# Infini-attention plus ReGLU on one core: one pool of PSUM banks, the token gate on VectorE, the memory in column tiles, and a plan with rings, queue and load times

## The chip, the core and the metric

The kernel runs on one core of one Trainium2 chip. The metric is the device time of one execution, in microseconds (us). Each time below is the median of four executions (of seven for the kernel before in the experiments), with the range in brackets. The profile is of one execution, and its "span" runs from the first to the last recorded instruction, which is about 2 us shorter than the device time. Engine names are those of the profile: PE is the matrix engine (TensorE), PEld its weight loads, DVE is VectorE, ACT is ScalarE, POOL is GpSimd, and SP is the engine whose queue issues most DMA transfers.

A run is called slow when it is over 1.5% above the fastest of the same kernel. The medians and ranges are of all runs; the three fast runs of the changed kernel have a median of 291.39 us.

## The reference

There are 2048 tokens of 512 features. An attention with a compressive memory (32 heads of 16, four segments of 512 tokens) and a gated ReLU feed-forward (1792 wide) are computed on the same input, and a scalar gate for each token mixes them:

```python
g = sigmoid((x * gate_w).sum(-1, keepdims=True))       # token gate: one number per token
a = infini_attention(x, wq, wk, wv, wo, beta)
b = (relu(x @ W_gate) * (x @ W_up)) @ W_down
return g * a + (1 - g) * b

# infini_attention, for each segment s of 512 tokens and each head
p   = softmax(qs @ ks.T * scale + causal_mask)
o   = sigmoid(beta) * (phi(qs) @ M) / (phi(qs) @ z + 1e-6) + (1 - sigmoid(beta)) * (p @ vs)
M, z = M + phi(ks).T @ vs,  z + phi(ks).sum()          # the memory, used by the next segment
```

## The kernel before

The kernel does not leave the order of instructions to a compiler. It makes a list of tasks, each with an engine, an estimated duration in ns, a priority and what it needs. It then simulates the engines and emits each task when the simulation starts it. **The order on every engine is fixed by this plan.** On the chip each engine executes its own list strictly in that order, and semaphores hold an instruction until its inputs are there. If a duration in the plan is wrong, the order stays, and the engines wait.

```python
class Plan:
    def run(self):
        ...                                            # cut: count what each task waits for
        for t in sorted((t for t in ready if t.avail <= now), key=rank):
            if busy.get(t.eng, 0.0) > now:
                continue
            ...                                        # cut: find a free PSUM bank
            if mode.get(t.eng) != t.mode:              # PE changes its tiling: a drain
                t.dur += SWITCH + (126 if t.mode and mode.get(t.eng) else 0)
            t.start = now
            busy[t.eng] = now + t.dur
            t.done = now + t.dur + t.lat
            order.append(t)
```

The kernel uses eight banks of PSUM. Four of them, `sp`, only ever hold scores, 32-row tiles that fill all four at once. One exponential of 128x2048 empties them ("fill" below means one such block of score matmuls; there are 80). Four single banks, `wb`, take all else. "Row tiles" are four matmuls that run side by side, each on 32 rows of PE's array; "column tiles" are the same on 32 columns each. An "eviction" is the instruction, mostly on VectorE, that copies a finished bank to SBUF and so lets PE use the bank again.

```python
sp = psum.tile([P, 4, L], F32, name="sp")
wb = [psum.tile([P, L], F32, name=f"wb{b}") for b in range(4)]
```

The token gate is computed by PE. 16 one-column matmuls give the sums of a segment, and a small fp32 matmul with a 0/1 matrix moves the gate values from "token on partition" to "four blocks of 32":

```python
def gate_tasks(seg):
    def pe():
        for t in range(4):
            for ci in range(NC):
                nc.tensor.matmul(bank(sl)[:, t:t + 1],
                                 lhsT=xT[seg % 3][:, ci, t * P:(t + 1) * P],
                                 rhs=gw[:, ci:ci + 1], ...)
    a = plan.add("PE", 420, key, pe, ...)
    ...                                                # cut: clamp, exponential, 1/(1+r), block mask
    d = plan.add("PE", 300, key, lambda: nc.tensor.matmul(
        bank(rsl)[:, 0:16], lhsT=fold[:]..., rhs=rblk[:]..., start=True, stop=True), ...)
```

The memory update is 16 full-array matmuls of 136 columns at the end of each of the first three segments:

```python
def memory(seg):
    for g in range(NC):
        for t in range(4):
            lo = (g % 2) * 136
            nc.tensor.matmul(wb[sl.banks[g // 2]][:, lo:lo + 136],
                             lhsT=pK[i][:, t, g * P:(g + 1) * P],
                             rhs=Vp[i][:, t, 8 * g:8 * g + 8, 0:HW], ...)
```

The softmax here doesn't subtract the row's maximum and nothing guards it: scores larger than these inputs give would overflow.

Of the kernel before, what the change touches and what calls it, by code (L numbers as in the profile page):

```python
# [12 lines left out]
P = 128  # L13
# [12 lines left out]
SWITCH = 100.0  # L26
RQ = 5
RE = 8
RH = 16


class Task:




    def __init__(self, eng, dur, key, emit, deps=(), lat=100, need=None, frees=(), after=None,
                 mode=None):
        self.eng, self.dur, self.key, self.emit, self.mode = eng, dur, key, emit, mode
        self.deps = [d for d in deps if d is not None]  # L40
        self.lat, self.need, self.frees, self.after = lat, need, tuple(frees), after
        self.avail = 0.0


class Slot:
    def __init__(self, kind):
        self.kind, self.banks, self.left = kind, (), 0


class Plan:  # L50



    def __init__(self, nbanks):
        self.tasks = []
        self.free = {i: 0.0 for i in range(nbanks)}

    def add(self, *a, **k):
        t = Task(*a, **k)
        self.tasks.append(t)  # L60
        return t

    def pick(self, slot, now):
        ok = [b for b in sorted(self.free) if self.free[b] is not None and self.free[b] <= now]
        if slot.kind == 2:
            for b in ok:
                if b % 2 == 0 and b + 1 in ok:
                    return (b, b + 1)
            return None
        for b in ok:  # L70
            if b ^ 1 not in ok:
                return (b,)
        return (ok[-1],) if ok else None

    def run(self):
        users = {}
        for t in self.tasks:
            t.wait = len(t.deps) + (t.after is not None)
            for d in t.deps:
                users.setdefault(id(d), []).append(t)  # L80
            if t.after is not None:
                users.setdefault(id(t.after), []).append(t)
            for s in t.frees:
                s.left += 1
        ready = [t for t in self.tasks if t.wait == 0]
        busy, mode = {}, {}
        now, order = 0.0, []
        left = len(self.tasks)
        while left:
            progressed = True  # L90
            while progressed:
                progressed = False
                def rank(t):
                    turn = t.mode and mode.get(t.eng) and t.mode != mode[t.eng]
                    return (bool(turn), t.key)
                for t in sorted((t for t in ready if t.avail <= now), key=rank):
                    if busy.get(t.eng, 0.0) > now:
                        continue
                    if t.need is not None and not t.need.banks:
                        got = self.pick(t.need, now)  # L100
                        if got is None:
                            continue
                        t.need.banks = got
                        for b in got:
                            self.free[b] = None
                    if mode.get(t.eng) != t.mode:
                        t.dur += SWITCH + (126 if t.mode and mode.get(t.eng) else 0)
                        mode[t.eng] = t.mode
                    t.start = now
                    busy[t.eng] = now + t.dur  # L110
                    t.done = now + t.dur + t.lat
                    order.append(t)
                    ready.remove(t)
                    left -= 1
                    for s in t.frees:
                        s.left -= 1
                        if s.left == 0:
                            for b in s.banks:
                                self.free[b] = t.done
                    for u in users.get(id(t), ()):  # L120
                        u.wait -= 1
                        u.avail = max(u.avail, t.start + t.dur if u.after is t else t.done)
                        if u.wait == 0:
                            ready.append(u)
                    progressed = True
            if not left:
                break
            times = [t.avail for t in ready if t.avail > now]
            times += [b for b in busy.values() if b > now]
            times += [f for f in self.free.values() if f is not None and f > now]  # L130
            assert times, "the plan is stuck"
            now = min(times)
        self.end = max(t.done for t in order)
        return order
# [3 lines left out]
def kernel(  # L138
# [21 lines left out]
    rpool = ctx.enter_context(tc.tile_pool(name="rpool", bufs=3))  # L160
    psum = ctx.enter_context(tc.tile_pool(name="psum", bufs=1, space=bass.MemoryType.PSUM))

    def sb(shape, dtype, name):
        return wpool.tile(shape, dtype, name=name)


    xT = [sb([P, NC, L], BF16, f"xT{i}") for i in range(3)]
    wq_sb = sb([P, NC, D], BF16, "wq_sb")
# [6 lines left out]
    gw = sb([P, NC], BF16, "gw")  # L175
    betab = sb([P, H], BF16, "betab")

    E = [sb([P, 4, L], BF16, f"E{i}") for i in range(RE)]
    x0 = E[RE - 1]
    clock = [3300.0]  # L180
    plan = Plan(4)

    def arrival(nbytes):
        clock[0] += nbytes / 340.0
        return plan.add("in%d" % len(plan.tasks), 0.0, 0.0, None, lat=clock[0])

    def load(eng, dst, src, nbytes):
        eng.dma_start(out=dst, in_=src)
        return arrival(nbytes)

    def load_cols(eng, t, ap, c0, c1):
        k = ap.shape[0] // P
        return load(eng, t[:, :, c0:c1], ap.rearrange("(c p) n -> p c n", p=P)[:, :, c0:c1],
                    k * P * (c1 - c0) * 2)

    def load_xT(seg):
        nc.sync.dma_start_transpose(out=xT[seg % 3][:], in_=x[seg * L:(seg + 1) * L, :])
        return arrival(L * D * 2 * 1.3)

    FP = [(0, 512), (512, 1024), (1024, 1408), (1408, F)]  # L200
    got_x, got_g, got_u = {}, {}, {}
    def load_halves(dst, src, k, nbytes):
        src = src.rearrange("(c p) n -> p c n", p=P)
        nc.sync.dma_start(out=dst[:, 0:k // 2], in_=src[:, 0:k // 2])  # L204
        nc.scalar.dma_start(out=dst[:, k // 2:k], in_=src[:, k // 2:k])
        return arrival(nbytes)

    got_x0 = load_halves(x0, x[0:L, :], 4, L * D * 2)
    got_q = [load_halves(wq_sb, A_wq, NC, D * D * 2)] * 2
    got_k = [load_cols(nc.sync, wk_sb, A_wk, 0, D)] * 2  # L210
    got_v = load_cols(nc.scalar, wv_sb, A_wv, 0, D)
    nc.scalar.dma_start(out=betab[:], in_=A_beta.partition_broadcast(P))
    with nc.allow_non_contiguous_dma(reason="1 KB"):
        nc.scalar.dma_start(out=gw[:], in_=gate_w.rearrange("(c p) -> p c", p=P))
    got_gw = arrival(0)

    def load_gu(i):
        got_g[i] = load_cols(nc.sync, wg_sb, B_W_gate, *FP[i])
        got_u[i] = load_cols(nc.sync, wu_sb, B_W_up, *FP[i])

    def load_wd(a, b):
        return load(nc.sync, wd_sb[:, a:b, :],
                    B_W_down.rearrange("(c p) n -> p c n", p=P)[:, a:b, :], (b - a) * P * D * 2)

    load_gu(0)
    load_gu(1)
    got_x[1] = [load_xT(1)]
    load_gu(2)
    load_gu(3)
    got_d = [load_wd(0, 7), load_wd(7, NF)]  # L230
    got_o = load_cols(nc.sync, wo_sb, A_wo, 0, D)
    got_x[2] = [load_xT(2)]


    junk = sb([P, L], BF16, "junk")
    nc.vector.memset(junk[:], 0.0)
# [16 lines left out]

    fold = sb([P, 4, 32], F32, "fold")
    nc.gpsimd.memset(fold[:], 0.0)
    pbm = sb([P, 4], F32, "pbm")
    nc.vector.memset(pbm[:], 0.0)
    for b in range(4):
        nc.gpsimd.affine_select(out=fold[:], in_=fold[:], compare_op=ALU.not_equal, fill=1.0,
                                base=-32 * b, pattern=[[0, 4], [-1, 32]], channel_multiplier=1)  # L260
        nc.vector.memset(pbm[32 * b:32 * b + 32, b:b + 1], 1.0)
    rblk = sb([P, 4, 4], F32, "rblk")
# [5 lines left out]
    grc = [sb([P, NC, 2, 2, 16], F32, f"grc{i}") for i in range(2)]  # L268

# [13 lines left out]

    sp = psum.tile([P, 4, L], F32, name="sp")
    wb = [psum.tile([P, L], F32, name=f"wb{b}") for b in range(4)]
    QT = [sb([P, L], BF16, f"QT{i}") for i in range(RQ)]
    KTe = [sb([P, L], BF16, f"KTe{i}") for i in range(RQ)]
    KTo = [sb([P, L], BF16, f"KTo{i}") for i in range(RQ)]
    pqT = [sb([P, L], BF16, f"pqT{i}") for i in range(RQ)]
    pK = [sb([P, 4, D], BF16, f"pK{i}") for i in range(2)]  # L290
    Vp = [sb([P, 4, H, 18], BF16, f"Vp{i}") for i in range(2)]
    oT = [sb([P, NC, L], BF16, f"oT{i}") for i in range(2)]
    hT = [sb([P, L], BF16, f"hT{i}") for i in range(RH)]
    T = [sb([P, 2, L], F32, f"T{i}") for i in range(2)]
    mbd = [sb([P, NC, 2, 4, 32], BF16, f"mbd{i}") for i in range(2)]
# [424 lines left out]
```

## Time and profile before

| | before |
|---|---|
| device time, us | 282.57 (282.07 to 282.74) |
| span of the profiled run, us | 280.8 |
| PE, DVE, ACT busy, us | 272.8, 205.7, 196.6 |
| idle of PE between its blocks, us | 4.2 |
| tiling changes of PE | 193, each a drain of 0.09 to 0.11 us |

The idle of PE and the drains are read from start-to-start times of the matmuls in the trace: a matmul of 512 columns is followed by the next after 216 ns when nothing is in the way. Idle counts each excess over 0.03 us beyond streaming and the usual drain; the 5.0 us of the prediction below counts the smaller ones too.

The first fence is the page of the kernel before: its span, the busy table, then two rows of busy tenths over 40 equal slices (9 is 90% or more), the granted clock of PE in tenths, and the shares of the chain of waits that ended last.

```profile
span 280.8 us, 5327 instructions
...
PE 272.8 (97%) x2122; PEld 113.4 (40%) x2122; DVE 205.7 (73%) x427; ACT 196.6 (70%) x176; POOL 87.6 (31%) x144
...
PE   8899999999989999999999999999999999999994
...
DVE  3588797798994768968997599957898966374221
...
PEclk9999999999999999999999999999999999999999
...
PE 92%; ACT 3%; DMA 3%; DVE 1%; issue 0%; SPq 0%; ACTq 0%
```

PE is full in every slice but the first two, one near 80 us and the last, and the chain of waits is PE for 92%. So time comes off this kernel only by taking work, drains or idle time from PE.

By start-to-start times a run of 16 one-column matmuls of the token gate takes 0.46 us, most often with a drain at its end. With the fold, the token gate costs PE 2.4 us in all. The three memory blocks cost 3.1 us. The last line is of the head gate, and will matter below: a small copy on 32 partitions, much like the 64 that the change adds, took 161 ns on VectorE.

The largest stall is early. In the timeline (start, duration, engine, line, operation; in brackets the idle time before it and what ended it) PE waits for `wk`, although two of its q projections, whose weights are there, are still to do:

```profile
9.55 1.25 PE L327 MATMUL wb<-xT,wk_sb 128*128 128x512 bf16 x5 [1.01 <-DMA wk_sb<-in_A_wk_dram]
```

The busy time of the engines in two stretches (stretch, its length, then busy us and number of instructions of PE, PEld, DVE, ACT and POOL, then the clock, the DMA share and GB/s):

```profile
0.00:115.00 115.00, 111.30 (x876) 46.26 (x877) 89.38 (x200) 87.69 (x82) 39.26 (x70) 1.00 0.38 101
115.00:275.00 160.00, 159.66 (x1240) 66.50 (x1239) 115.57 (x228) 108.88 (x95) 48.33 (x74) 1.00 0.04 12
```

### The profile page before, as it was taken

The numbers are of one execution on the slowest core, as the hardware profiler recorded it, in microseconds if no ns is written. First come the engines' busy times: TensorE is split into PE (matmuls) and PEld (weight loads), VectorE is DVE, ScalarE is ACT, GpSimd is POOL, SyncE is SP. The second block draws the span as 40 slices with busy tenths as digits, with TensorE's granted clock in tenths as the row PEclk, the third lists the DMA queues.
The fourth block names the chain that finished last, engine by engine and source line by source line (L and its number), as shares of the span: only waits on it lengthen the run. The fifth ranks groups of instructions, "written<-read, shape, count | busy, mean of one in ns | idle before, by whom it ended". The sixth has DMA issues, their size and how long they took to land.

```text
span 280.8 us, 5327 instructions
## 1 busy us (share of the span) xinstructions
PE 272.8 (97%) x2122; PEld 113.4 (40%) x2122; DVE 205.7 (73%) x427; ACT 196.6 (70%) x176; POOL 87.6 (31%) x144
## 2 busy tenths in 40 slices
PE   8899999999989999999999999999999999999994
PEld 3343444433434343343443344344434343444441
DVE  3588797798994768968997599957898966374221
ACT  3299797988886659888876779898897677723000
POOL 7014233334242332433343424443334243300000
PEclk9999999999999999999999999999999999999999
DMA  7999930013001010000001000000000010000011
GB/s 230 316 255 349 208 49 19 4 22 75 19 2 39 21 37 2 19 2 19 0 11 47 21 21 2 0 2 0 2 0 2 19 39 21 0 2 0 0 37 39
DMA packets 24488, 13.71 MB, mean 49 GB/s; under 512 B 13968, under 2 KB 24464, under 8 KB 24464
## 3 DMA queue, kind: packets, MB, share of 16 engines
q1 hardware_dynamic: 22720, 12.32, 16.5%
q10 hardware_dynamic: 1744, 1.06, 1.3%
q8 instruction: 16, 0.26, 0.4%
q14 instruction: 8, 0.07, 0.1%
HBM read 8.14 MB, written 2.10 MB: 36 GB/s over the span
## 4 chain that ended last, share of the span: by engine, by line
PE 92%; ACT 3%; DMA 3%; DVE 1%; issue 0%; SPq 0%; ACTq 0%
PE wb L327 73%; PE sp L478 9%; PE wb L518 7%; DMA wk_sb<-in_A_wk_dram 3%; ACT E L499 2%; PE wb L574 2%; PE wb L592 1%; ACT rg L628 1%; PE wb L360 1%; SPq L204 0%; DVE osb L658 0%; DVE T L547 0%; PE wb L380 0%; ACT e L416 0%; ACTq L628 0%
## 5 line engine op out<-in xcount | busy, mean ns | idle before, releaser
L499 ACT ACTIVATE E<-sp 128x2048 bf16<-128x2048 f32 x80 | 150.4, 1880 | 37.0 <-PE sp L478 33.0
L505 POOL TENSOR_SCALAR_AFFINE_SELECT E<-E 128x512 bf16<-128x512 bf16 x128 | 82.5, 660 | 156.0 <-ACT E L499 156.0
L327 PE MATMUL wb<-xT,wg_sb 128*128 128x512 bf16 x224 | 59.7, 380 | 0.0
L327 PE MATMUL wb<-xT,wu_sb 128*128 128x512 bf16 x224 | 59.3, 380 | 0.4 <-ACT rg L628 0.4
L327 PE MATMUL wb<-wd_sb,hT 128*128 128x512 bf16 x224 | 54.1, 380 | 0.0
L635 DVE TENSOR_TENSOR hT<-wb,rg 128x512 bf16<-128x512 f32 x56 | 38.1, 682 | 17.7 <-PE wb L327 9.7
L547 DVE STREAM_TRANSPOSE T<-wb 128x512 f32<-128x512 f32 x56 | 36.7, 693 | 14.9 <-PE wb L518 9.0
L628 ACT ACTIVATE rg<-wb 128x512 bf16<-128x512 f32 x56 | 33.0, 602 | 13.8 <-PE wb L327 13.8
L327 PEld LDWEIGHTS <-hT 128*128 128x128 bf16 x224 | 20.4, 98 | 26.1 <-issue 4.2
L327 PEld LDWEIGHTS <-wu_sb 128*128 128x128 bf16 x224 | 20.3, 98 | 26.2 <-issue 5.0
L327 PEld LDWEIGHTS <-wg_sb 128*128 128x128 bf16 x224 | 19.8, 98 | 25.3 <-issue 5.5
L658 DVE TENSOR_SCALAR osb<-wb,ngcol 128x512 bf16<-128x512 f32 x16 | 11.9, 741 | 17.7 <-PE wb L327 17.6
L558 DVE TENSOR_TENSOR o<-T,cf 128x512 bf16<-128x512 f32 x28 | 20.1, 718 | 1.0
L518 PE MATMUL wb<-E,Vp 128*17 128x256 bf16 (+3 forms) x512 | 20.4, 300 | 0.0
L478 PE MATMUL sp<-QT,KTo 32*128 32x512 bf16 (+3 forms) x256 | 17.1, 299 | 0.8 <-ACT E L499 0.8
L478 PE MATMUL sp<-QT,KTe 32*128 32x512 bf16 (+3 forms) x256 | 17.3, 302 | 0.3 <-ACT E L499 0.3
L327 PE MATMUL wb<-xT,wk_sb 128*128 128x512 bf16 x64 | 16.5, 380 | 1.0 <-DMA wk_sb<-in_A_wk_dram 1.0
L327 PE MATMUL wb<-wo_sb,oT 128*128 128x512 bf16 x64 | 17.1, 380 | 0.0
L327 PE MATMUL wb<-wv_sb,xT 128*128 128x512 bf16 x64 | 16.8, 380 | 0.2 <-DVE T L547 0.2
L327 PE MATMUL wb<-xT,wq_sb 128*128 128x512 bf16 x64 | 16.7, 380 | 0.1
L408 DVE CAST QT<-wb 128x512 bf16<-128x512 f32 x16 | 11.0, 688 | 6.8 <-PE wb L327 4.4
L518 PEld LDWEIGHTS <-Vp 128*17 128x17 bf16 x512 | 10.7, 91 | 13.0 <-issue 4.2
(70 smaller groups left out, 192.9 us busy)
## 6 DMA issues: line engine op xcount, KB each, us to landing
out_dram<-osb SPq DMA_DIRECT2D x16, 128.0 KB, 1.7
wd_sb<-in_B_W_down_dram SPq DMA_DIRECT2D x2, 896.0 KB, 8.4
wg_sb<-in_B_W_gate_dram SPq DMA_DIRECT2D x2, 512.0 KB, 9.6
wu_sb<-in_B_W_up_dram SPq DMA_DIRECT2D x2, 512.0 KB, 10.0
wg_sb<-in_B_W_gate_dram SPq DMA_DIRECT2D x2, 384.0 KB, 5.2
wu_sb<-in_B_W_up_dram SPq DMA_DIRECT2D x2, 384.0 KB, 5.2
wk_sb<-in_A_wk_dram SPq DMA_DIRECT2D x1, 512.0 KB, 7.7
wv_sb<-in_A_wv_dram ACTq DMA_DIRECT2D x1, 512.0 KB, 9.1
```

The source lines that it names most:

```text
L327: nc.tensor.matmul(bank(sl), lhsT=lhsT, rhs=rhs, start=(start and q == 0), stop=(stop and q == n - 1))
L408: prj["q", seg, c] = plan.add("DVE", 690, key - RQK, lambda: nc.vector.tensor_copy(QT[i][:], bank(sl)), [a], DVL, frees=[sl])
L478: nc.tensor.matmul(sp[:, j, off:off + n], lhsT=kt[32 * j:32 * j + 32, kb * P:(kb + 1) * P], rhs=QT[i][32 * j:32 * j + 32, kb * P:kb * P + ...
L499: b = plan.add("ACT", 1880, key, lambda Ef=Ef: nc.scalar.activation(Ef[:], sp[:], ACT.Exp, scale=SCALE), [a] + eread.get(n - RE, []), ACL)
L505: nc.gpsimd.affine_select(out=m, in_=m, compare_op=ALU.is_ge, fill=0.0, base=0, pattern=[[0, 4], [1, P]], channel_multiplier=-1)
L518: nc.tensor.matmul(wb[sl.banks[0]][32 * j:32 * j + HW, kb * P:kb * P + w], lhsT=Vp[i][:, kb, 8 * c + 2 * j + r, 0:HW], rhs=E[(5 * u + f) % ...
L547: done.append(plan.add("DVE", 700, key - RL, lambda r=r, sl=sl: nc.vector.transpose(T[m][:, r], bank(sl)), [a, att.get(("part", m, u - 1)) ...
L558: nc.vector.tensor_tensor(dst[0].rearrange("p (q r e) -> p r q e", r=2, e=DH), t[:, :, :, 0:DH], cf[:, :, :, None].to_broadcast([P, 2, 16, ...
L574: a = plan.add("PE", 216, key + r, lambda r=r, sl=sl: nc.tensor.matmul(bank(sl), lhsT=mbd[i][:, c, r].rearrange("p j e -> p (j e)"), rhs=p ...
L628: nc.scalar.activation(rg[0][:], bank(sl), ACT.Relu)
L635: nc.vector.tensor_tensor(hT[(NF * seg + fv) % RH][:], bank(sl), rg[0][:], ALU.mult)),
L658: nc.vector.tensor_scalar(osb[0][:], bank(sl), ngcol[:, tt:tt + 1], None, ALU.mult)
```

## The change

The intent was to take the small work off PE and to have a better plan. The diff is long; its core, with cuts marked, follows.

1. The token gate moves to VectorE: a multiply-and-sum pass over the rows of x, which are loaded a second time, and 16 small copies per segment in place of the fold matmul.
2. The memory becomes 64 column-tile matmuls of 34 columns, tied to a block of the probability-times-value product (PV), which uses column tiles too.
3. PSUM becomes one pool of eight banks. The four score banks may be lent to other work between fills.
4. The plan knows buffer rings, the sync queue and a table of measured load times. Many task durations are reduced. A block of column tiles is ranked later while PE is in row tiles, and a score fill may follow a PV block directly.
5. A table of 132 shifts, found by a search against the plan, changes the priority of single tasks.
6. The last output tile is computed in two halves.

```diff
+SHIFT = {
+    29: 30000, 32: 310000, 48: 80000, ...            # cut: 132 entries in all
+}
...
-    sp = psum.tile([P, 4, L], F32, name="sp")
-    wb = [psum.tile([P, L], F32, name=f"wb{b}") for b in range(4)]
+    plan.pool("ps", 8)
+    ps = psum.tile([P, 8 * L], F32, name="ps")
...
+    LANDS = dict(n0=4500, q=5950, k=9300, v=9750, g0=11800, u0=13300, gw=13700, g1=15200, u1=16700,
+                 x1=18400, g2=20400, u2=21600, g3=22800, u3=24000, d0=27700, d1=30400, o=31800)
...
+    plan.add("SP", 23300, -1e9, None)                # the sync queue is busy with loads until here
...
 def gate_tasks(seg):
-        a = plan.add("PE", 420, key, pe, got_x[seg] + [got_gw], PEL, need=sl)
+        for t in range(4):
+            zs.append(plan.add("DVE", 640, key, lambda t=t: nc.vector.scalar_tensor_tensor(
+                junk[:], xn[seg % 2][:, t, :], 1.0, gwb[:], ALU.mult, ALU.mult,
+                accum_out=zc[:, 4 * seg + t:4 * seg + t + 1]), [got_n[seg], got_gw], 60))
...
-        d = plan.add("PE", 300, key, lambda: nc.tensor.matmul(
-            bank(rsl)[:, 0:16], lhsT=fold[:].rearrange("p j q -> p (j q)"), ...
+        def spread():
+            for j in range(4):
+                for b in range(4):
+                    nc.vector.tensor_copy(rq[seg % 2][32 * j:32 * j + 32, :, b],
+                                          rcol[32 * b:32 * b + 32, cols])
+        d = plan.add("DVE", 1050, key, spread, [c, att.get(("gate", seg - 2))], 60)
...
 def memory(seg, u):
+                    for j in range(4):
+                        nc.tensor.matmul(
+                            bank(sl)[32 * j:32 * j + 32, 34 * g:34 * g + 34],
+                            lhsT=pK[i][:, t, g * P + 32 * j:g * P + 32 * j + 32],
+                            rhs=Vp[i][:, t, 8 * g + 2 * j:8 * g + 2 * j + 2, 0:HW],
+                            ..., tile_position=(0, 32 * j))
...
+            got_n[seg] = plan.add("SP", 520, KA(4 * seg - 4), lambda seg=seg: load_xn(seg),
+                                  att.get(("xn", seg - 2), []), 3500)
...
+    for n, d in SHIFT.items():
+        plan.tasks[n].key += d
     order = plan.run()
```

## The prediction

> **What bounds the kernel now.** The busy table gives PE 97% of a 280.8 us span, DVE 73%, ACT 70%; the chain of waits is PE for 92%. So PE time counts. By start-to-start times in the timeline, 512-column matmuls follow each other every 216 ns; streaming alone (score and PV tiles four at once) sums to about 238 us. The rest:
>
> - First useful matmul at 5.45 us; 4.0 us from the last matmul's end to the span's end (a 0.75 us eviction, then the store).
> - 80 score blocks (row tiles) and 17 PV blocks (column tiles), each entered and left with a drain of 116 to 132 ns: about 23 us. The Trainium skill (TensorEngine Tiling, Key Properties) says that changing the tiling mode drains the array; the trace agrees, with those numbers.
> - Token gate: four runs of 16 one-column matmuls, 0.46 us each, and four pairs of fp32 fold matmuls, 0.14 us: 2.4 us.
> - Memory: three blocks of 16 matmuls of 136 columns, 3.1 us.
> - True stalls, 5.0 us: 1.2 at 8.2 us (for wk, although two q projections were left to do), 1.0 at 79 (a fill waits for the exponential), 0.4 at 49 and 130, 0.3 at 112 (bank held by VectorE), and small ones.
>
> **What the change does.**
>
> 1. Token gate to VectorE: PE loses 2.4 us. DVE gains 16 multiply-and-sum passes (estimate 0.65 us, as its other one-a-cycle 512-column instructions) and 64 small copies (about 0.1 us each): about +15 us, mostly off the path. Gain 2.4.
> 2. Memory in column tiles behind a PV block: 64 matmuls of 34 columns. PV's 128-column quartets advance every 55 ns; estimate 30 to 50 ns a round, so 0.5 to 0.8 us per block against 1.04. Gain 1.3.
> 3. One pool of eight banks, real load times, rings and queue in the plan: aims at the stalls. The wk stall should vanish, most others shrink: 5.0 to about 1.5. Gain 3.5.
> 4. A score fill may directly follow PV, which was ranked down: one drain, 0.12 us, saved each time; estimate 8 times. Gain 1.0. The 80 score blocks stay 80, since each exponential still takes all four banks. This keeps the largest overhead, 20 us.
> 5. Last tile in halves: the last eviction falls from 0.75 to about 0.4 us. Gain 0.4.
> 6. Costs: x loaded a second time (2 MB; DMA is near idle after 50 us); lent score banks can delay a fill, and so the exponentials (ACT is busy about 80% from 10 to 200 us); DVE goes to some 80%. I allow 0.5.
>
> Sum: about -8, nearly all on PE.
>
> **Prediction: 274.5 us** (from 282.57), range 271 to 279. Chances: faster by over 2% 0.77, within 2% 0.20, slower 0.03.
>
> **What would show each step right.** No one-column and no fp32 matmuls on PE. Memory blocks under 0.8 us. No wait for wk over 0.3 us near 8 us. Still 80 score blocks with 110 to 130 ns on each side, a handful fewer drains. PE stalls under 2 us in sum. DVE busy 215 us or more. Exponentials still 80 of 1.88 us. Last matmul ends about 3.5 us before the span's end.
>
> **What would make it wrong.** Weight loads of 32 columns slower than I think; an order that fits a model rather than the chip, so that stalls move instead of shrinking (then 277 to 279); VectorE late with evictions because of the gate passes; or reordering that joins score and PV blocks much more often than eight times (then 271 or 272).

## More of the kernel before

The groups of instructions (line, engine, operation, out<-in, shapes, count | busy us, mean ns of one | idle before) show what the token gate and the memory cost on PE:

```profile
L592 PE MATMUL wb<-Vp,pK 128*128 128x136 bf16 x48 | 3.5, 226 | 0.0
L360 PE MATMUL wb<-gw,xT 128*128 128x1 bf16 x64 | 2.2, 163 | 0.0
L380 PE MATMUL wb<-rblk,fold 128*128 128x16 f32 x8 | 1.2, 221 | 0.0
...
L273 DVE COPY ebq<-eb 32x8 f32<-32x8 f32 x4 | 0.6, 161 | 0.0
```

Matmuls overlap, so a mean of 163 ns for a one-column matmul is its time in the pipeline and not its cost: they start 25 ns apart.

## The result, and the profile after

| | before | after |
|---|---|---|
| device time, us | 282.56 (282.07 to 282.74) | 292.16 (289.96 to 294.36) |
| span of the profiled run (fast), us | 280.8 | 289.1 |
| PE busy, us | 272.8 | 272.0 |
| DVE busy, us | 205.7 | 221.9 |
| idle of PE between its blocks, us | 4.2 | 17.6 |

The ratio is 1.032, with a 95% interval of 1.028 to 1.037: the kernel became slower by 3.2%. Ratios are the mean time of one kernel's fast runs over that of the other's in the same rounds, so they are not quite the ratios of the quoted medians.

The page of the changed kernel, with the same lines as before:

```profile
span 289.1 us, 5565 instructions
...
PE 272.0 (94%) x2212; PEld 113.5 (39%) x2212; DVE 221.9 (77%) x512; ACT 196.7 (68%) x176; POOL 88.2 (31%) x139
...
PE   8997496998899999999999999999999999999995
...
DVE  3789799899999999979979877658897772946322
...
PEclk9999998999999999999999999999999999999999
...
PE 59%; DVE 20%; DMA 6%; ACT 5%; SPq 5%; issue 3%; ACTq 0%; DVEq 0%
```

The chain of waits was nearly all PE. Now it is DVE for 20%, DMA for 6% and the sync queue for 5%. PE's row has holes in slices 4 to 11, and the DVE row is nearly full just there. The two stretches again:

```profile
0.00:115.00 115.00, 101.59 (x807) 41.17 (x808) 99.88 (x273) 79.60 (x77) 36.13 (x60) 0.99 0.43 114
115.00:275.00 160.00, 159.39 (x1338) 65.79 (x1337) 118.85 (x235) 117.11 (x100) 52.09 (x79) 1.00 0.04 11
```

**The whole loss lies before 115 us.** There PE is busy 101.59 us against 111.30, and DVE 99.88 against 89.38. After 115 us PE is as full as before. The four token gates all run before 108 us.

The groups answer to those shown of before:

```profile
L410 DVE COPY rq<-rcol 32x4 f32<-32x4 f32 x64 | 13.1, 204 | 0.8
L393 DVE SCALAR_TENSOR_TENSOR junk<-xn,gwb 128x512 bf16<-128x512 bf16 x16 | 11.6, 725 | 2.0 <-DMA xn<-in_A_x_dram 1.9
L652 PE MATMUL ps<-Vp,pK 128*32 128x34 bf16 x192 | 2.0, 183 | 0.0
L393 DVE DVE_READ_ACCUMULATOR junk<-xn,gwb 128x1 f32 x16 | 1.3, 81 | 0.0
```

The gate on PE is gone and the memory is smaller: 1.48 us by start-to-start times, against 3.11. On VectorE the copies cost 204 ns each in the mean. The plan counts 1050 ns for 16 of them, which is 66 ns each. Sixteen in a row take 3.56 us, 222 ns each.

That mean mixes two kinds (shortest, median and longest of the 64 copies, then GpSimd's work during the first sixteen, which start at 25.37 us):

```profile
L410 DVE COPY rq<-rcol x64: 127/163/581, 25.4 to 107.4; 32x4 f32<-32x4 f32 x64
```

```profile
25.90 1.23 POOL L565 TENSOR_SCALAR_AFFINE_SELECT E<-E 128x512 bf16<-128x512 bf16 x2 [2.83 <-ACT E L556]
```

57 of the copies take at most 168 ns and start about 175 ns apart. The other seven take 520 to 581 ns. Each of the seven started while GpSimd was at a mask, and ended 20 to 23 ns after that mask did; none of the 57 started during one. In each of xn_early, no_shift, true_times and before_gate below it is again seven of 64, all started during a mask, ended 17 to 24 ns after it, and again none of the others. So 16 copies take about 2.8 us by themselves (an estimate from 175 ns each), and waiting for GpSimd's masks adds 0.4 to 0.8 us.

Two stretches of the timeline show how this reaches PE. The first is around 33 us. VectorE waits 1.91 us for the second segment's x rows. The evictions that PE needs stand behind that wait in the queue, and so PE waits 3.01 us for an eviction that has nothing to do with the gate:

```profile
33.59 0.69 DVE L393 SCALAR_TENSOR_TENSOR junk<-xn,gwb 128x512 bf16<-128x512 bf16 x1 [1.91 <-DMA xn<-in_A_x_dram]
...
34.94 1.28 DVE L693 TENSOR_TENSOR hT<-ps,rgr 128x512 bf16<-128x512 f32 x2
```

```profile
35.68 0.72 PE L578 MATMUL ps<-E,Vp 128*17 128x512 bf16 x16 [3.01 <-DVE hT L693]
```

This load was issued at 24.65 us, while the weights were still coming in, and landed at 33.56, after 8.9 us. The plan gives it 3.5 us, plus 0.52 us to issue. The Trainium skill (DMA: Bandwidth & Descriptors, "Issuing engines are not separate DMA queues") says that all transfers run on the same 16 DMA engines and interleave. The trace agrees: the three x loads of this size have a median of 3.9 us from issue to landing, and this one, issued among the weights, took 8.9.

The second stretch is around 45 us. The 16 copies hold VectorE for 3.57 us. Behind them stands a k cast, then the rest that lets a bank go, and PE is idle for 2.37 us:

```profile
43.31 3.57 DVE L410 COPY rq<-rcol 32x4 f32<-32x4 f32 x16
46.91 0.69 DVE L490 CAST ktr<-ps 128x512 bf16<-128x512 f32 x1
```

```profile
44.87 1.04 PE L427 MATMUL ps<-xT,wq_sb 128*128 128x512 bf16 x4
48.28 1.01 PE L427 MATMUL ps<-xT,wu_sb 128*128 128x512 bf16 x2 [2.37 <-ACT ex L466]
```

The releaser named is ScalarE, which ended last; what held both ScalarE and PE is the busy VectorE queue. Look also at the last line's count: two matmuls took 1.01 us where four took 1.04. The same engines by stretch say why. The column after POOL is the clock:

```profile
44.90:48.30 3.40, 1.03 (x9) 0.39 (x6) 3.23 (x13) 0.66 (x2) 0.54 (x1) 0.98 0.00 0
48.30:51.70 3.40, 3.40 (x8) 1.00 (x7) 2.75 (x8) 2.19 (x2) 1.14 (x2) 0.52 0.00 0
51.70:55.00 3.30, 2.98 (x45) 1.35 (x45) 2.49 (x7) 3.05 (x4) 0.72 (x2) 1.00 0.21 40
```

After a stretch of 3.4 us in which PE worked for 1.03 us, the next 3.4 us ran at half clock, which costs another 1.7 us. PE counts as fully busy there. So the busy share is no measure of progress here. The Trainium skill (Perfetto Trace Analysis, "Identifying the Most-Contended Engine") warns that it is not a good measure for PE, for another reason: pipelined instructions look smaller in the trace. PE's busy time is 272.8 us before and 272.0 after, for a kernel that takes 8.3 us longer and has less work on PE. A longer gap in the same trace, the 3.01 us that end at 35.68 us, was not followed by a lower clock: 1.00 in the 3.4 us after it.

**The sum.** By start-to-start times in both traces:

| step | us |
|---|---|
| token gate off PE | -2.4 |
| memory 1.48 against 3.11 | -1.6 |
| 178 tiling changes against 193, at about 0.10; PV block straight to score fill 14 times against 1 | -1.4 |
| last matmul's end to span's end 3.06 against 3.97 | -0.9 |
| idle of PE 17.6 against 4.2; about 1.4 of it is matmuls at half clock after 48.3 us, which start too far apart | +13.4 |
| first transposes of x at half clock in this run, 1.73 against 0.90 | +0.8 |
| sum (the span grew by 8.3) | +7.9 |

Every intended saving of work and of drains arrived. The idle time of PE ate them and more.

One more reading is used below. The plan has its own start time for every fill, so the chip's lag behind the plan can be followed fill by fill (us; only the larger steps are shown):

```
fill   plan   chip    lag   step since the fill before
   0   12.7   13.4   0.72   0.72
   4   24.4   26.3   1.90   1.23
   5   27.4   30.7   3.21   1.31   (16 copies at 25.4)
   6   30.0   36.3   6.34   3.13   (wait for x rows)
  10   41.3   51.7  10.42   4.14   (16 copies at 43.3, then half clock)
  17   60.9   74.0  13.06   2.32   (16 copies at 67.4)
  21   71.8   85.5  13.72   0.71
  31   98.6  113.8  15.18   0.77   (16 copies at 104.0)
  79                15.54          (last fill)
```

Between the gates the chip follows the plan to within some hundredths of a microsecond per fill: fills 1 to 3 and 7 to 9 add 0.02 us or less each. The plan ends at 272.9 us. So the chip could do what the plan asks wherever the gate was not in the way, and it lost most of the 15 us at the gates. The four lumps of 16 copies took 3.56, 3.57, 3.17 and 3.57 us.

### The profile page after: what moved, and what is told of

Same layout as the page of the kernel before. It is cut to its first block, busy times and chain, and to the rows that moved or that the text cites. A ratio compares the mean times of both kernels' runs of the same rounds, so it can differ in the third digit from the quotient of the medians.

```text
span 289.1 us, 5565 instructions
## 1 busy us (share of the span) xinstructions
PE 272.0 (94%) x2212; PEld 113.5 (39%) x2212; DVE 221.9 (77%) x512; ACT 196.7 (68%) x176; POOL 88.2 (31%) x139
## 4 chain that ended last, share of the span: by engine, by line
PE 59%; DVE 20%; DMA 6%; ACT 5%; SPq 5%; issue 3%; ACTq 0%; DVEq 0%
PE ps L427 47%; PE ps L536 6%; PE ps L578 4%; DVE rq L410 3%; DMA xn<-in_A_x_dram 3%; DMA wv_sb<-in_A_wv_dram 3%; SPq L284 3%; DVE T L608 3%; ACT E L556 2%; SPq L297 2%; DVE junk L393 2%; ACT ex L466 2%; PE ps L634 2%; DVE hT L693 2%; DVE ktr L490 1%
## 5 line engine op out<-in xcount | busy, mean ns | idle before, releaser
L556 ACT ACTIVATE E<-ps 128x2048 bf16<-128x2048 f32 x80 | 150.5, 1881 | 38.4 <-PE ps L536 31.2
L427 PE MATMUL ps<-xT,wu_sb 128*128 128x512 bf16 x224 | 58.1, 384 | 4.9 <-ACT ex L466 2.4
L427 PE MATMUL ps<-xT,wg_sb 128*128 128x512 bf16 x224 | 58.8, 380 | 1.3 <-DVE hT L693 1.1
L427 PE MATMUL ps<-wd_sb,hT 128*128 128x512 bf16 (+1 forms) x238 | 54.7, 367 | 0.2 <-DVE osr L715 0.2
L693 DVE TENSOR_TENSOR hT<-ps,rgr 128x512 bf16<-128x512 f32 x56 | 37.8, 682 | 11.2 <-PE ps L427 6.8
L608 DVE STREAM_TRANSPOSE T<-ps 128x512 f32<-128x512 f32 x56 | 37.2, 694 | 9.1 <-PE ps L578 5.4
L687 ACT ACTIVATE rgr<-ps 128x512 bf16<-128x512 f32 x56 | 33.2, 604 | 15.6 <-PE ps L427 14.2
L427 PEld LDWEIGHTS <-wu_sb 128*128 128x128 bf16 x224 | 20.7, 98 | 32.0 <-issue 10.0
L578 PE MATMUL ps<-E,Vp 128*17 128x256 bf16 (+3 forms) x512 | 21.2, 300 | 4.3 <-DVE hT L693 3.7
L619 DVE TENSOR_TENSOR och<-T,cfr 128x512 bf16<-128x512 f32 x28 | 19.6, 701 | 0.4
L427 PE MATMUL ps<-xT,wk_sb 128*128 128x512 bf16 x64 | 18.1, 395 | 0.9 <-DVE T L608 0.9
```

The costliest lines, as they stand in the source:

```text
L427: nc.tensor.matmul(bank(sl)[:, 0:width], lhsT=lhsT, rhs=rhs, start=(start and q == 0), stop=(stop and q == n - 1))
L556: nc.scalar.activation(Ef[:, e0 * L:e1 * L], ps[:, e0 * L:e1 * L], ACT.Exp, scale=SCALE),
L578: nc.tensor.matmul(bank(sl)[32 * j:32 * j + HW, kb * P:kb * P + w], lhsT=Vp[i][:, kb, 8 * c + 2 * j + r, 0:HW], rhs=E[(NFILL * u + f) % RE ...
L608: done.append(plan.add("DVE", 633, key - RL, lambda r=r, sl=sl: nc.vector.transpose(T[ts.i][:, r], bank(sl)), [a] + done, DVL if r else 0, ...
L619: nc.vector.tensor_tensor(och[ds.i].rearrange("p (q r e) -> p r q e", r=2, e=DH), t()[:, :, :, 0:DH], cfr[cs.i][:, :, :, None].to_broadcas ...
L687: r = plan.add("ACT", 478, key - RL, lambda sl=gsl, rs=rs: nc.scalar.activation(rgr[rs.i][:], bank(sl), ACT.Relu), [g], ACL, frees=[gsl])
```

## The experiments

The theories, as the expectations below call them:

- **A**: the token gate on VectorE is the loss. VectorE works in the plan's order, the plan's times for the gate's work and its load are too short, VectorE falls behind, and PE waits for evictions behind it. Its two variants are **A1**, that the wrong times in the plan are what hurts, and **A2**, that the added work is simply too much for VectorE, whatever the plan is told.
- **B**: the loss comes from the rest of the change, the new order, the lent banks or the queue; its variant **B'** is that the table of shifts was fitted to the plan and hurts on the chip.

All kernels were compared with the kernel before in the same rounds on the same chip; that kernel had medians of 282.2 to 282.7 us throughout. All results are correct except where a wrong result was intended.

| run | median, us | ratio to before (95%) |
|---|---|---|
| six_copies | 286.49 (283.67 to 287.03) | 1.012 (1.006 to 1.017) |
| spread_pool | 289.04 (288.06 to 289.36) | 1.022 (1.019 to 1.025) |
| xn_early | 288.38 (287.49 to 289.74) | 1.021 (1.017 to 1.025) |
| before_gate | 303.24 (301.85 to 303.98) | 1.071 (1.067 to 1.076) |
| no_gate (wrong) | 277.11 (276.98 to 277.78) | 0.981 (0.980 to 0.983) |
| six_xn | 280.39 (280.32 to 280.88) | 0.993 (0.991 to 0.994) |
| no_shift | 293.98 (292.99 to 294.62) | 1.041 (1.040 to 1.043) |
| true_times | 284.02 (283.90 to 284.07) | 1.005 (1.004 to 1.007) |
| best_base | 290.39 (288.85 to 290.77) | 1.028 (1.025 to 1.031) |
| best_table | 284.23 (283.99 to 284.30) | 1.007 (1.005 to 1.008) |
| pe_gate_base | 289.12 (288.88 to 290.62) | 1.025 (1.022 to 1.029) |
| queue_table | 280.63 (280.35 to 281.41) | 0.993 (0.991 to 0.995) |

The granted clock has to be read beside these times. Stretches at half clock, 3.4 or 6.8 us long, appear in the traces of the kernels with long idle of PE. The mean granted clock is 1.000 in every execution of no_gate, six_xn and queue_table and at least 0.998 in those of true_times and best_table, but 0.982 or 0.983 in all of no_shift, 0.988 in three of four of six_copies, and 0.994, 0.977, 1.000 and 0.988 in the four of the changed kernel (0.977 is the slow one). An estimate of the time lost, span times the missing share of the clock, is 5 us for no_shift, 3 to 7 for before_gate, 2 to 4 for spread_pool, 3.4 for six_copies, 2 to 3.5 for best_base and pe_gate_base, up to 3.5 for the fast runs of the changed kernel and of xn_early, and none for six_xn. It differs between executions of one kernel, so it is not the wait itself.

### 1. Fewer copies, same order (six_copies)

```diff
-            for j in range(4):
-                for b in range(4):
-                    nc.vector.tensor_copy(rq[seg % 2][32 * j:32 * j + 32, :, b],
-                                          rcol[32 * b:32 * b + 32, cols])
+            r = rq[seg % 2]
+            for b in range(4):
+                nc.vector.tensor_copy(r[0:32, :, b], rcol[32 * b:32 * b + 32, cols])
+            nc.vector.tensor_copy(r[32:64], r[0:32])
+            nc.vector.tensor_copy(r[64:128], r[0:64])
```

> The changed kernel with the same order on every engine; the spread of the gate takes 6 VectorE copies in place of 16 (same values, right result). In the changed kernel's trace a spread takes 3.2 to 3.6 us of VectorE's queue where the plan had 1.05. Theory A (VectorE falls behind the fixed order in the gates: evictions queue behind them and TensorE waits): three of the spreads come down to about 1.2 us, TensorE stalls fall from 17.6 to some 10 us, time 292 to about 284 to 286. Theory B (the new order and the banks do not fit the chip, whatever the gate costs): within 1 us of the changed kernel, 291 to 293.

It took 286.49 us, somewhat more than A expected, and about 5.7 us less than the changed kernel (ratios 1.012 and 1.032). The plan, and so the order of all instructions, is unchanged. The copies at 25.4 us now take about 1.8 us instead of 3.56 (DVE lines of the timeline of this run):

```profile
25.39 0.65 DVE L410 COPY rq<-rcol 32x4 f32<-32x4 f32 x4
26.07 0.51 DVE L411 COPY rq<-rq 32x16 f32<-32x16 f32 x1
26.62 0.56 DVE L412 COPY rq<-rq 64x16 f32<-64x16 f32 x1
...
33.14 0.69 DVE L393 SCALAR_TENSOR_TENSOR junk<-xn,gwb 128x512 bf16<-128x512 bf16 x1 [3.58 <-DMA xn<-in_A_x_dram]
```

PE's idle fell from 17.6 to 13.3 us. The last line tells why the gain was not larger: the load of x lands at 33.1 us, hardly earlier than before (33.6), so VectorE arrives earlier and waits longer, 3.58 us against 1.91. One delay had hidden the other. After this longer wait the clock is at half from 34.6 to 41.4 us, one slice (7.1 us) of the page's clock row:

```profile
PEclk9999959999999999999999999999999999999999
```

### 2. The same copies on GpSimd (spread_pool)

```diff
-                    nc.vector.tensor_copy(rq[seg % 2][32 * j:32 * j + 32, :, b],
+                    nc.gpsimd.tensor_copy(rq[seg % 2][32 * j:32 * j + 32, :, b],
                                           rcol[32 * b:32 * b + 32, cols])
```

> The changed kernel with the same order; the 16 copies are issued by GpSimd (31% busy) and not by VectorE. Theory A: VectorE busy time falls by about 13 us, the spread steps vanish altogether, time 282 to 285, a little below the one with six copies, unless GpSimd's masks come late. Theory B: 291 to 293.

This expectation missed: 289.04 us. GpSimd takes 212 ns per copy, no less than VectorE, and it too has an order to keep (POOL lines, then DVE lines, of the timeline of this run):

```profile
44.84 3.61 POOL L410 COPY rq<-rcol 32x4 f32<-32x4 f32 x16
48.52 1.52 POOL L565 TENSOR_SCALAR_AFFINE_SELECT E<-E 128x512 bf16<-128x512 bf16 x2
```

```profile
46.06 0.69 DVE L490 CAST ktr<-ps 128x512 bf16<-128x512 f32 x1 [0.40 <-PE ps L427]
48.48 0.42 DVE L414 TENSOR_TENSOR grc<-rq,gcat 128x256 f32<-128x256 f32 x1 [1.73 <-POOL rq L410]
```

The masks of the exponentials stand behind the copies on GpSimd, and VectorE still waits for the copies' result in its own order. Taking the work off VectorE without changing what VectorE waits for next moves the block to another queue. That is not all of the miss: as in six_copies, VectorE now waits longer for x (2.63 us), the lag steps by 4.44 and 2.02 us at fills 6 and 7, and the clock is at half from 34.0 to 40.8 us.

### 3. The second x load before the large weights (xn_early)

```diff
     load_gu(3)
+    load_xn(1)
     got_d = [load_wd(0, 7, "d0"), load_wd(7, NF, "d1")]
...
-            got_n[seg] = plan.add("SP", 520, KA(4 * seg - 4), lambda seg=seg: load_xn(seg),
+            got_n[seg] = plan.add("SP", 520, KA(4 * seg - 4), (lambda ...) if seg > 1 else None,
```

> The changed kernel, same order, all 16 copies; only the second segment's load of x is issued before the loads of W_down, not after them. In the changed kernel VectorE stands idle 1.9 us at 31.7 us for this load, and the seventh score fill is 3.1 us later against the plan than the sixth. Theory A (in-order VectorE, any wait in the gate counts): that step goes, 2 to 3.5 us less, 288.5 to 290. Theory B: no change beyond 1 us.

288.38 us, close to what was expected. VectorE no longer waits for x, and the lag's step at fill 6 falls from 3.13 to 1.13 us. The steps of the copies remain (1.31 at fill 5, 3.98 at fill 10). By the ratios (1.032 and 1.021) the load alone is worth about 3 us of the loss, or 2.2 us when only executions at full clock are compared (289.96 against 287.49 and 288.07).

### 4. Only the gate moved, in the kernel before (before_gate)

The kernel before keeps its order, its banks and its times. Its two PE tasks of the gate emit nothing, and the passes and 16 copies are emitted where the small VectorE tasks were. The second segment's x is loaded early, as in xn_early.

```diff
         def pe():
-            for t in range(4):
-                for ci in range(NC):
-                    nc.tensor.matmul(bank(sl)[:, t:t + 1], ...)
+            pass
...
+        def token():
+            xs = xn if seg else x0
+            for t in range(4):
+                nc.vector.scalar_tensor_tensor(junk[:], xs[:, t, :], 1.0, gwb[:], ...)
+            nc.vector.tensor_scalar(zc[:, cols], zc[:, cols], 80.0, -80.0, ALU.min, ALU.max)
...
         def blk():
-            nc.vector.tensor_tensor(rblk[:], ...)
+            for j in range(4):
+                for b in range(4):
+                    nc.vector.tensor_copy(rq[32 * j:32 * j + 32, :, b], rcol[32 * b:32 * b + 32, cols])
```

> The kernel before, its order and its banks kept, with only the token gate's work moved to VectorE (4 multiply-and-sum passes and 16 copies per segment; second segment's x loaded early). TensorE has 2.4 us less work. Theory A: VectorE late by about 6 us at four places, of which some is absorbed by its idle time: 285 to 291, slower than 282.6. Theory B: 280 to 283, the gate alone does no harm.

303.24 us, 20.7 more than before. The direction is A's, the size is far beyond what A expected. Nothing of the rest of the change is in this kernel, and PE has 2.4 us less to do. PE's idle is about 28 us, most of it at the four gates, and three stretches (near 63, 148 and 223 us) run at about half clock. Here the plan knows nothing at all of the added work (it thinks of 170 ns where 3.6 us run), so the order is further from the chip's times than in the changed kernel. B alone cannot explain this run.

### 5. The changed kernel without the gate's work (no_gate)

Passes, copies and the second loads of x are left out; the plan still counts them, so the order is that of the changed kernel. The gate's tiles are set to 0.5 once. The result is wrong (relative error 0.62).

```diff
-            zs.append(plan.add("DVE", 640, key, lambda t=t: nc.vector.scalar_tensor_tensor( ...
+            zs.append(plan.add("DVE", 640, key, None, [got_n[seg], got_gw], 60))
...
         def spread():
-            for j in range(4): ...
+            pass
```

> Wrong result on purpose: the changed kernel, same order, but the 16 multiply-and-sum passes, the 64 copies and the later loads of x for them are left out (the gate is a constant). It shows what the rest of the change is worth. If the gate on VectorE is the whole loss (theory A): TensorE stalls under 3 us, time 274 to 277, faster than before by over 2%. If pool, order and rings also cost (theory B): 280 or more.

277.11 us: all else in the change is worth 1.9%, and the gate on VectorE costs 5.2% on top (1.032 over 0.981), about 14.3 us, with what it does to the clock. The lag behind the plan ends at 1.10 us, against 15.54. This rejects B: the new order, the banks and the queue are followed almost exactly, shifts and all, once VectorE is on time.

### 6. Both repairs together, same order (six_xn)

Edits 1 and 3 in one kernel.

> Changed kernel, same order, six copies and the second segment's x loaded early: both mends together. The run with six copies alone still waited 3.6 us for the load, so the mends should add up to more than 5.7 + 3.8: theory A says 280 to 283.5; what is left is the passes themselves, 0.73 us each where the plan had 0.64, and a 1.3 us stall at 23 us. If the two waits are independent of each other: 283.

280.39 us, correct, and 0.7% faster than before. By the ratios the two repairs gain about 5.7 and 3.2 us alone and 11 together (1.032 against 0.993), which looks like more than the sum. Most of that is the clock: it was at half for part of both single repairs and never here. Net of the estimate above, the gains are 6.3 and 2.5 us alone and 9.2 together, so that the rest is too small for four executions to show. VectorE is still busy 213.6 us, and the clock of PE is 1.000. The lag ends at 5.08 us. This speaks against A2: the passes are all still there, and most of the loss is gone.

### 7. Without the table of shifts (no_shift), and with true times in the plan (true_times)

```diff
-    for n, d in SHIFT.items():
+    for n, d in ():
```

true_times has this edit and three more; the work done on the chip is that of no_shift, instruction for instruction, in another order:

```diff
-            zs.append(plan.add("DVE", 640, key, ...
+            zs.append(plan.add("DVE", 735, key, ...
...
-        d = plan.add("DVE", 1050, key, spread, ...
+        d = plan.add("DVE", 3560, key, spread, ...
...
-                                  att.get(("xn", seg - 2), []), 3500)
+                                  att.get(("xn", seg - 2), []), 8900 if seg == 1 else 3500)
```

> The changed kernel with the table of shifts of priorities empty, planned anew with the same times. Theory B' (the table of shifts fits a model and hurts on the chip): faster than the changed kernel, below 288. Theory A: the gate's times are as wrong as before, so about 289 to 296, no better.

> As the one with the empty table, but the plan is told what the trace shows: 3.56 us for a spread, 0.735 us for a pass, 8.9 us until the second x load lands. The work on VectorE is the same. If the loss is work that the plan does not know of (A1), the plan can put it where VectorE has time: 279 to 284. If VectorE simply has too much to do early on (A2): over 287, like the empty table.

no_shift took 293.98 us, true_times 284.02, **10 us less with the same 64 copies, 16 passes and loads**. About half of the 10 us is the clock, which was at half from 22.9 to 29.7 and from 53.6 to 57.0 us in no_shift and never in true_times (the first row is of no_shift's page):

```profile
PEclk9995999799999999999999999999999999999999
...
PEclk9999999999999999999999999999999999999999
```

In no_shift the steps are where the gates are, for instance (PE and DVE lines of its timeline):

```profile
24.27 0.58 PE L427 MATMUL ps<-xT,wg_sb 128*128 128x512 bf16 x1 [3.46 <-DVE hT L693]
```

```profile
19.86 3.63 DVE L410 COPY rq<-rcol 32x4 f32<-32x4 f32 x16
23.52 0.69 DVE L693 TENSOR_TENSOR hT<-ps,rgr 128x512 bf16<-128x512 f32 x1
```

In true_times no step of the lag is over 0.6 us, and the lag ends at 2.58 us. This is the run that decides between A1 and A2: the work fits, if the plan knows how long it takes. It also rejects B': without the table the kernel is slower than with it (1.041 against 1.032), so the table did not cause the loss. And it gives the price of the slow copies even when planned for: the true plan ends at 279.0 us, against 272.9 as the plan stood. no_shift's plan, with the short times and no table, ends at 275.6, so the true times are 3.4 us of the difference and the missing table 2.7.

### 8. Plans made anew for the better gate (best_base, best_table, pe_gate_base)

best_base takes six_xn's gate, tells the plan 1250 ns for the copies, 740 ns for a pass and 25 us for the landing of x, and has no shifts. best_table adds a searched table of 82 shifts. pe_gate_base is the new plan with the token gate back on PE, without shifts.

```diff
-SHIFT = { ... }
+SHIFT = {}
+    LANDS = dict(n0=4500, n1=25000, ...
...                                                    # cut: load_xn(1) early, the six copies
-            zs.append(plan.add("DVE", 640, ...
+            zs.append(plan.add("DVE", 740, ...
...
-        d = plan.add("DVE", 1050, key, spread, ...
+        d = plan.add("DVE", 1250, key, spread, ...
```

> Six copies, second x early, the plan told their real times (1.25 us a spread, 0.74 us a pass, x at 25 us), empty table of shifts. In the earlier runs with true times the chip lagged the plan by 2.6 us at the last score fill. The plan's end here is 3.0 us earlier than in the run with true times and 16 copies, so 281, and at least 2 us under that run's 284.0. If the number of copies did not matter once the plan knows them: 284.

> The same with a table of 82 shifts searched against the plan with those times; the plan's end is 3.2 us earlier. If the chip follows the plan as it did in the kernels with true times: 277 to 279, faster than the kernel before by 1.2 to 2% and faster than every right kernel so far. If such a table only fits the model: no better than the one with the empty table.

> The new plan with the token gate on TensorE as in the kernel before, empty table: only this part of the change undone. TensorE works 2.4 us more than in the one with the gate on VectorE. If moving the gate pays once its copies are few and its times known: 2 us slower than that one, about 283. If the gate is better left on TensorE: 280 or less.

All three missed: 290.39, 284.23 and 289.12 us. For best_base and pe_gate_base the traces show the same theory with another culprit. In best_base, at fill 6, the lag jumps by 5.92 us. VectorE waits for a DMA again, but not for x (DVE line, then PE line, of its timeline):

```profile
33.43 0.29 DVE L444 TENSOR_SCALAR pkT<-ktr 128x512 bf16<-128x512 bf16 x1 [3.76 <-DMA pK<-pkT]
```

```profile
34.84 1.25 PE L561 MATMUL ps<-E,Vp 128*17 128x512 bf16 x16 [4.83 <-DVE hT L676]
```

The transposes of the keys go through the sync queue, behind the weight loads. The plan says that the queue is free from 23.3 us; on the chip the transposes issued at about 26 us are not through until 33. A three-deep ring (`pkT`) is then full, VectorE waits to write into it, and the evictions wait behind. pe_gate_base has the same jump (5.07 us at the same fill), so **it does not tell whether the gate is better on PE, and that stays open**. In best_table the lag is 8.66 us in many small steps, which fits a table searched against times that leave no room, but is not shown to come from that.

### 9. The queue in the plan (queue_table)

best_table's kernel, with the sync queue blocked until 31 us in the plan, all VectorE durations raised by 4%, and a table of 54 shifts searched for this plan.

```diff
-    plan.add("SP", 23300, -1e9, None)
+    plan.add("SP", 31000, -1e9, None)
...
-        self.eng, self.dur, self.key, self.emit, self.mode = eng, dur, key, emit, mode
+        self.eng, self.key, self.emit, self.mode = eng, key, emit, mode
+        self.dur = dur * 1.04 if eng == "DVE" else dur
```

> As the one with the searched table, but the plan also knows that the sync queue is blocked until 31 us (in the runs with empty or new tables VectorE waited 3.8 to 6.1 us there for transposes of the keys queued behind the weight loads), and takes VectorE's times 4% longer, to leave room; table searched anew. If unknown times are what makes the chip lag the plan: no jump over 1.5 us at the sixth or seventh score fill, a lag of 3 to 5 us at the last one, time 279 to 282, below the searched table's 284.2. If the lag comes from elsewhere: 284 or more.

280.63 us, correct. The jump at fill 6 is gone, the largest step is 1.40 us (fill 4), and the lag ends at 3.53 us. Two changes and a new table were made together, so their shares are not separated. six_xn and queue_table both beat the changed kernel, and the kernel before by 0.7%, by two ways: work made short enough for the plan, and a plan made long enough for the work.

## Why the prediction was wrong

The prediction was 274.5 us, range 271 to 279. The result is 292.16.

1. **"Token gate to VectorE ... about +15 us, mostly off the path. Gain 2.4." This step failed.** The size of the work was right in sum: VectorE's busy time grew by 16.2 us. Within it a pass was near (estimated 0.65 us, measured 0.725 and 0.081 for the read of the accumulator, 0.73 from start to start), and a copy was half of what it is (estimated 0.1 us, measured 0.204 in the mean, 0.163 in the median). What failed is "mostly off the path". The work comes in lumps of 3.2 to 3.6 us, four times, in a queue where PE's evictions stand behind it. The chain of waits went from 1% to 20% VectorE. No_gate puts the price at about 14.3 us.
2. "Memory in column tiles ... Gain 1.3" was right, and 1.6 was measured. A block takes 0.49 us against an estimate of 0.5 to 0.8.
3. **"Aims at the stalls ... 5.0 to about 1.5. Gain 3.5." This failed with the first step.** The wait for wk did vanish. The idle of PE became 17.6 us, some 1.4 of it matmuls at half clock. The step trusted the plan's load times and durations. Three of them were wrong: the copies 1.05 us against 3.56, the second x load 3.5 against 8.9, and the time when the sync queue is free. With the gate's work gone the plan was kept (no_gate: lag 1.10 us), and with true times mostly too (true_times: 2.58). So the third step's mechanism works only as far as the plan's times are the chip's times.
4. "A score fill may directly follow PV ... estimate 8 times. Gain 1.0" was right in kind and under-sized: 13 more direct passages, and about 1.4 us of drains less in all. The 80 score blocks stayed 80, as said. The Trainium skill (TensorEngine Tiling, Key Properties) that the step rests on agrees again: each of the 66 changes from full tiles to row tiles costs at least 0.092 us by start-to-start times, with a median of 0.096.
5. "Last tile in halves ... Gain 0.4" was under-sized: 0.9 us. The last eviction takes 0.48 us against 0.75, and the store behind it is smaller too.
6. "Costs: x loaded a second time (DMA is near idle after 50 us) ... I allow 0.5" was mis-sized. The load that hurt is the one at 24.65 us and not those after 50. Early, it costs 3.01 us of PE's idle where VectorE waits for it. The worry about lent score banks was needless. In the plan of the changed kernel, of the work allocations six got a score bank and all others one of the four work banks; lending is hardly used.

The list of what could go wrong did name "VectorE late with evictions because of the gate passes", and gave slower only 3%. The warning was not followed to numbers. The numbers were at hand. VectorE was 73% busy over the whole span before, but 83% from 20 to 50 us (25.02 of 30 us), where two of the gates were to go. And the trace of before had nearly the same instruction: the four copies of the head gate, 32x8 on 32 partitions each, take 161 ns in the mean and start 172 ns apart. Sixteen at that pace are 2.75 us, where the plan had 1.05 and the prediction 1.6.

What stays open: whether the gate is better left on PE with a plan of true times. The step of 1.2 us at fill 4, near 25 us, which six_copies, spread_pool, xn_early and six_xn share with the changed kernel, can be read in its trace: a pass of the first gate at 22.51 us stands in front of the eviction that PE waits for, and took 1.11 us and not 0.69. It too overlaps a mask on GpSimd; in no_gate the pass is not there, nor is the step. (In queue_table the step there is made of waits of PE for ScalarE, 0.44 and 0.84 us.) For the 175 ns from copy to copy, the Trainium skill (VectorE: DVE Perf Modes, "Two Vector instructions with no wait between them") offers a part of a cause, as a model: an instruction whose input or output starts in another quadrant of 32 partitions than the last one's is held until all earlier Vector instructions have finished. Each of the 16 copies changes a quadrant, and in the trace none starts before the one in front has ended. But no run here kept the quadrants, so it is not shown.

## What to carry to other kernels

In a kernel with a fixed order, work moved to an engine "with time to spare" is not free: ask what stands behind it in that engine's queue, how long the longest lump is, and who waits for the thing behind it. Take every duration in a plan from a trace of the same shape on the same engine, small instructions and loads that share the DMA engines above all; the same work cost 10 us less when the plan was told the truth. When one delay is removed, look for the next one behind it before judging the repair: with fewer copies the wait for x grew from 1.91 to 3.58 us. Compare the granted clock of two kernels before giving a difference to a cause; here it was about half of the 10 us.

## What the Trainium skill lacked or had wrong

- TensorE: Matmul & The Clock Gate, Part 1, puts the loss of clock after an idle window of about 3.4 us, and its rule warns of idle gaps above that. Here a single idle gap of 2.37 us, in a stretch of 3.4 us with PE busy for 1.03 us, was followed by 3.4 us at 0.52 of full clock. A gap that costs the clock can be shorter than the rule says, and a longer one, 3.01 us at 32.7 us in the same trace, left it at 1.00; what decides it, these runs do not show.
- The same page, Part 1, says that the start-to-start time of matmuls never drops below about 25 ns, and Part 3 lets packed tiles start about 4 ns apart. One-column full-array matmuls here agree with the floor (25 ns from start to start). In column tiles 64 matmuls of 34 columns took 0.49 us, 7.7 ns each or about 31 ns for a round of four. So the floor looks like one per round of tiles; the page does not say which it is.
- TensorEngine Tiling (Array Packing), Key Properties, says that a change of mode drains and gives no figure. They cost 0.09 to 0.11 us in these traces, which for the 193 changes of the kernel before comes to about 19 us of 280.8.
- VectorE: DVE Perf Modes, TRN2 errata: its table gives 58 cycles plus the columns for a small SBUF instruction, which is an estimate of 65 ns for four columns at its 0.96 GHz and close to what the plan had. The text under the table says that the row is too low, with a measured fixed term of about 150 cycles, an estimate of 160 ns. The copies of 32x4 agree with the text (median 163 ns) and not with the table.
- No page prices the read of an accumulator (81 ns each here).
- No page prices a small copy on GpSimd: the same 32x4 copy took 212 ns there in the mean, 186 in the median.
